# Attention and feed-forward block, eight more slots of lead for the row scores, six key tiles, untied weight loads, one staging tile

## The chip, the core and the metric

The kernel runs on one core of one Trainium2 chip. The core has a matrix engine (PE), a vector engine (DVE), a scalar engine (ACT), a general engine (POOL) and a sync engine (SP), which here issues every DMA. Each takes its instructions in order and waits on semaphores. Arithmetic is float32, and matrix products use the float32r form with operands split into a high and a low part. The metric is device time in microseconds (us) of one launch, lower is better.

## What is computed

A transformer block over 2048 rows of 576 features: a modulated layer norm, attention with 32 heads of 18 features, a residual, a second modulated layer norm, a feed-forward of 4608 features, a residual.

```python
mod = (silu(c) @ w_mod)            # sa, ca, ga, sb, cb, gb
h = layernorm(x) * (1 + ca) + sa
q, k, v = split_heads(h @ wqkv)    # 32 heads of 18
p = softmax(q @ k.T * 18 ** -0.5)
x = x + ga * (merge_heads(p @ v) @ wo)
h = layernorm(x) * (1 + cb) + sb
x = x + gb * (silu(h @ w1) @ w2)
```

## The kernel before

**Stages.** The 2048 query rows are cut into four blocks of 512. A block has eight quads, and a quad is four heads of one block. In the trace the stages are: the start (0 to about 152 us), the attention of block 0 (to about 618), the attention of blocks 1, 2 and 3 (to about 1197, 1715 and 2205), and a tail with the feed-forward of block 3. The output projection, second norm and feed-forward of a block (`post`, L888) are cut into filler pieces that run between the attention slots of the next block. In block 0 the filler is the remaining query and key projections (`qk_one`, L563, 24 of them, 14 matmuls each).

**Slots.** A quad has 32 slots. Each slot is done twice over, in two passes.

- Pass a, row scores (`slot_a`, L739, matmul at L735): two matmuls give the scores of 128 queries against 512 keys for two heads in banks `psa`, three of which exist, and DVE takes the row maximum of each (`mx`, L737). After the 32nd slot of a quad `max_a` (L749) joins the maxima and `max_rows` (L760) sends them by DRAM (`mscr`) into two spare rows of the quad's query tile `qt`. Eight slots share one chunk of 512 keys, held in two of four tiles `ka`.
- Pass b, exponentials (`slot_b`, L768, matmul at L785): two matmuls give the scores of 128 keys against 512 queries, less the row maximum through the two spare rows, in banks `psb`. ACT writes the exponentials to one of the tiles `pt`. The keys of a chunk of eight slots lie in two of four tiles `kb`.

Pass b of slot s runs beside pass a of slot s + `LEAD`, with `LEAD` 40, so the maxima of a quad are finished eight slots before its first exponential. The first 40 slots of pass a lie in the start. The last 40 slots of pass b have no pass a beside them.

**Values.** When both head pairs of a key tile (128 keys) have their exponentials, `pv` (L815) multiplies them with the values. Up to `PVMAX` = 5 key tiles go in one run. A key tile holds two `pt` tiles. There are seven `pt` tiles in block 0 and three more afterwards (`PB = 7, 10`, L60 and L865). `room` (L1508) keeps the planner from starting a slot when all are taken.

**Loads of keys.** `slot_load` (L717) loads `ka` and the query tiles, `slot_b` (L773) loads `kb`: in slot 8n + 2 and 8n + 4 the tiles of chunk n + 1. These take the place of chunk n - 1, which pass b left at slot 8n. A query tile (`load_quad`, L681, three buffers) asks first that the filler has projected its heads (`need`, L675): what is missing runs at once, without slots between.

**Weights.** `weights` (L643) prepares split weights on their first use. It loads half a tile to `raw` (three buffers), POOL writes high and low parts, and the result is stored in DRAM (`w1s`, `w2s`, `wos`) at the next call (`store_rest`, L638). For the first layer and the output projection this happens in block 0 through a staging tile `we` (`early`, L633, two buffers, 41 tiles). For the second layer it happens on first use by the feed-forward of block 0, which runs in the attention of block 1, straight into the tiles `w2t` (five buffers). POOL there does three passes for each half: times the gate (L654), cast (L655), difference (L656). Later blocks load the stored parts (L647). `after_pe` (L457) makes a DMA wait for the last exponentials' score matmul that stands before it in the program. It is on all first loads (L652) and their stores (L641), and not on the loads of stored parts.

**Order.** The order on PE is written by a planner with fixed costs (`Plan`, L99, and the loop from L1498): it chooses among a slot, a run of values and a piece of filler. Filler is paced evenly over the slots: in block 0 over 2 x 236 half slots from the loop's start (L1496). The other engines and SP get their order from the framework's scheduler: an instruction is placed when, by the scheduler's own clock, what it needs is ready, with program order as priority. The start has a list scheduler of its own (`Start`, L191) with priorities for all engines.

```python
        if j == 0:
            if s >= 8 and s % 8 in (2, 4):
                load_k("b", s // 8 + 1, s % 8 // 2 - 1)
...
            after_pe(nc.sync.dma_start(raw, src[:, cs]))
```

Of the kernel before, what the change touches and what calls it, by code (L numbers as in the profile page):

```python
# [18 lines left out]
P = 128  # L19
# [17 lines left out]
SCALE = DH ** -0.5  # L37
EPS = 1e-5
QM, KM, XM = 0, 1, 2
LEAD = 40  # L40
CH = 4


# [13 lines left out]
LP0 = 1000  # L57
REST = (16, 8, 0, 0)
LP = 2000
PB = 7, 10  # L60
PVMAX, PVMIN = 5, 3
QKB = 3
GS = 2
# [27 lines left out]
def f(ap):  # L91
    return ap.bitcast(F32)
# [98 lines left out]
class Start:  # L191
# [18 lines left out]
    def dma(self, size, fn, deps=(), prio=0, take=(), free=()):  # L210
        return self.add("D", size / self.RATE, fn, deps, prio, take, free)
# [128 lines left out]
def tile_adaln_block(ctx: ExitStack, tc: tile.TileContext, x, wqkv, wo, w1, w2, c, wfirst, wcol, out):  # L340
# [12 lines left out]

    at1 = ctx.enter_context(tc.tile_pool(name="at1", bufs=1))
    kas = [at1.tile([P, 512], F32R, name=f"ka{i}") for i in range(4)]
    kbs = [at1.tile([P, 512], F32R, name=f"kb{i}") for i in range(4)]

    ident = const.tile([P, P], F32, name="ident")
    make_identity(nc, ident)
# [97 lines left out]
    def after_pe(ins):  # L457
        if state["pe"] is not None:
            tc.add_manual_dep(ins.ins, state["pe"].ins.name, SYNC, reason="its turn by the plan")
# [171 lines left out]
                        fill.add(200, lambda a=mt_: mod_piece(*a), mode="full")  # L631

    def early(src, scr, gate=None):  # L633
        weights(mp["e"].tile([P, 2, 640], F32R, tag="w", name="we", bufs=2)[:, :, :src.shape[1]], src, scr, True, gate)

    stores = []

    def store_rest():  # L638
        while stores:
            w, scr = stores.pop()  # L640
            after_pe(nc.sync.dma_start(f(scr), f(w)))  # L641

    def weights(w, src, scr, first, gate=None):  # L643

        store_rest()
        if not first:
            nc.sync.dma_start(f(w), f(scr))  # L647
            return
        n = w.shape[2] // 2
        for cs in (slice(0, n), slice(n, 2 * n)):  # L650
            raw = mp.get("p", mp.get("e")).tile([P, 320], F32, tag="raw", name="raw", bufs=3)[:, :n]
            after_pe(nc.sync.dma_start(raw, src[:, cs]))  # L652
            if gate is not None:
                nc.gpsimd.tensor_tensor(raw, raw, gate[:, cs], op=ALU.mult)  # L654
            nc.gpsimd.tensor_copy(w[:, 1, cs], raw)  # L655
            nc.gpsimd.tensor_tensor(w[:, 0, cs], raw, f(w[:, 1, cs]), op=ALU.subtract)  # L656
        stores.append((w, scr))
# [39 lines left out]
    def load_k(ring, n, hp):  # L697
        i, kc = divmod(n, NKEY)
        if i >= NQ:
            return  # L700
        kt_ = (kas if ring == "a" else kbs)[n % 2 * 2 + hp]
        h = 4 * (i % NQUAD) + 2 * hp
        for j in range(2):
            nc.sync.dma_start(f(kt_[64 * j:64 * j + 54, :]),
                              f(kscr[(h + j) * DH:(h + j + 1) * DH, :, kc * 512:(kc + 1) * 512].rearrange("d c s -> (d c) s")))
        quads.setdefault(i, {})[ring, kc, hp] = kt_
# [9 lines left out]

    def slot_load(s):  # L717
        i = s // 32
        if s % 32 == (22 if i == 0 else 14) and i + 1 < NQ:
            load_quad(i + 1)  # L720
        n, w = divmod(s, 8)
        if w == 1:
            if s == LEAD + 1:
                load_k("a", n + 1, 0)
            load_k("a", n + 1, 1)
        elif w == 5:
            load_k("a", n + 2, 0)
# [40 lines left out]
    def slot_b(s, j):  # L768
        i, w = divmod(s, 32)
        kt, hp = divmod(w, 2)  # L770
        t = quads[i]
        if j == 0:
            if s >= 8 and s % 8 in (2, 4):  # L773
                load_k("b", s // 8 + 1, s % 8 // 2 - 1)
            if w == 0:
                t["P"] = {}
            if w == 16 and i + 1 < NQ:
                load_v(i + 1)
            state["p"] += 1
            t["P"][kt, hp] = pts[0]  # L780
            pts.append(pts.pop(0))

        e = 1 - j
        ps = bank_b("psb")
        state["pe"] = mm(ps, lhsT=t["b", kt // 4, hp][64 * e:64 * e + 56, kt % 4 * P:(kt % 4 + 1) * P],  # L785
           rhs=t["q"][64 * e:64 * e + 56, hp, :], start=True, stop=True)
        nc.scalar.activation(t["P"][kt, hp][:, e, :], ps, AF.Exp, scale=SCALE)  # L787
        at = t.setdefault(("exp", kt), [])
        rel = plan.take("b")

        def done(at_):
            rel(at_)
            at.append(at_ + TR)
        plan.op("A", plan.t + TL - TS + 30, TEXP, done)
        if hp == 1 and j == 1:
            pend.append((i, t, kt, at))
# [324 lines left out]
    def start_tasks(st):  # L1121
# [282 lines left out]
        k_in = {}  # L1404
        ones_t = []
        t = dma(16e3, lambda: nc.sync.dma_start(f(oscr.rearrange("r (a s) -> r a s", a=NKT)), full[0:2, None, :].to_broadcast([2, NKT, P])), prio=4.2)
        for n in range(8):
            ones_t.append(dma(40e3, lambda n=n: nc.sync.dma_start(f(kbs[n // 2][64 * (n % 2) + 54:64 * (n % 2) + 56, :]), f(oscr[:, :512])), [t], 8.4))
        q_in = [dma(443e3, lambda: load_quad(0), stored[QM, 0, 0], 5.5)]
        for kc in range(4):  # L1410
# [3 lines left out]
        mm_t = None  # L1414
        for s in range(LEAD):
            i, w = divmod(s, 32)
            if s in (24, 32):
                kc = s // 8 - 3
                k_in[1, kc] = dma(443e3, lambda kc=kc: [load_k("a", 4 + kc, hp) for hp in range(2)], stored[KM, 0, kc] + stored[KM, 1, kc] + [mm_t, k_in[(0, 3) if kc == 0 else (1, 0)]], 10 if kc else 8.8)
            ka = tok("a", 2)  # L1420

            def both(s=s):
# [192 lines left out]
```

## Time and profile before

| what | value |
|---|---|
| runs | 2488.22, 2495.07, 2496.23 us, median 2495.07 |
| profiled execution | 2487.03 us, of which 2485.2 us is the span of its instructions |
| granted PE clock over the span | 0.977 |
| DMA | 459.56 MB, 185 GB/s on average |

The span is what the views of the profile cover. The remaining 1.8 us of the profiled execution lie around it. A row of a group gives its line in the kernel, engine, operation, result and operands, count, and after the bar the busy time in us, the mean duration in ns and the engine's idle time before it with what ended it. In the view of stretches each engine's busy time in us is followed by the count of instructions, and then the clock granted to PE (1.00 is full speed), the busy share of the 16 DMA engines and GB/s. In the timeline a row is start, duration, engine, line, operation, operands and the count of merged instructions, with the idle time before it in brackets.

### The profile page before, as it was taken

What the parts mean: (1) busy time and instruction counts of PE and PEld (TensorE: products, weight loads), DVE (VectorE), ACT (ScalarE), POOL (GpSimd) and SP (SyncE); (2) the same over time, 40 slices, a digit from 0 to 9 for tenths busy, and PEclk for the clock granted to TensorE, in tenths of its full rate; (3) what the DMA queues carried; (4) which work ended last, traced back from release to release, by engine and by line L of the source; (5) the groups of instructions that cost most, each with busy time, mean ns of one, the idle gap of its engine ahead of it and who ended that gap; (6) DMA issues with size and microseconds to landing.
All of it is one profiled execution on the core that took longest, in us unless ns stands there. A gap on an engine that the chain in (4) does not pass through costs nothing.

```text
span 2485.2 us, 52362 instructions
## 1 busy us (share of the span) xinstructions
PE 2369.4 (95%) x19952; PEld 1625.0 (65%) x19952; DVE 1785.8 (72%) x3110; ACT 1483.6 (60%) x2736; POOL 631.1 (25%) x763
## 2 busy tenths in 40 slices
PE   6999998998999999999999999999999999989999
PEld 5863343433666667666667767776676677678988
DVE  8887786887777778777788777887888778234333
ACT  5246675776566666666577677776677667732121
POOL 5213343421343444344221111112211111120000
PEclk9999998999999999998999999999999999999999
DMA  7767776755355565555455555444654454326563
GB/s 251 247 199 237 255 256 219 260 192 181 128 168 174 176 198 182 172 167 170 158 184 166 187 177 174 165 157 160 209 180 159 158 182 165 131 102 238 173 219 119
DMA packets 208003, 459.56 MB, mean 185 GB/s; under 512 B 32010, under 2 KB 68266, under 8 KB 207754
## 3 DMA queue, kind: packets, MB, share of 16 engines
q1 hardware_dynamic: 207754, 456.21, 55.2%
q8 instruction: 160, 2.62, 0.4%
q14 instruction: 89, 0.73, 0.1%
HBM read 365.07 MB, written 86.33 MB: 182 GB/s over the span
## 4 chain that ended last, share of the span: by engine, by line
PE 79%; DMA 7%; DVE 5%; POOL 3%; ACT 2%; issue 2%; SPq 1%; POOLq 0%; ACTq 0%; DVEq 0%
PE ps L483 24%; PE psv L822 16%; PE psa L735 12%; PE ps L477 10%; PE psb L785 8%; DMA raw<-in_w 4%; PE psqk L569 3%; DVE mx L737 2%; PE psv L483 2%; PE psp L483 1%; DMA kb<-kscr 1%; POOL raw L654 1%; PE psqk L483 1%; POOL w2t L655 1%; POOL w2t L656 1%
## 5 line engine op out<-in xcount | busy, mean ns | idle before, releaser
L737 DVE TENSOR_REDUCE mx<-psa 128x1 f32<-128x512 f32 x2048 | 1320.8, 684 | 364.6 <-PE psb L785 206.9
L787 ACT ACTIVATE pt<-psb 128x512 f32<-128x512 f32 x2048 | 1131.1, 598 | 554.6 <-PE psb L785 350.0
L785 PE MATMUL psb<-qt,kb 56*128 56x512 f32 x2048 | 760.6, 431 | 29.1 <-DMA kb<-kscr 9.9
L735 PE MATMUL psa<-ka,qt 54*128 54x512 f32 x2016 | 704.7, 422 | 9.8 <-DVE mx L737 8.1
L735 PEld LDWEIGHTS psa<-ka,qt 54*128 54x128 f32 x2016 | 339.3, 189 | 308.9 <-DVE mx L737 207.6
L822 PE MATMUL psv<-pt,vt 128*32 128x512 f32 x4096 | 518.8, 610 | 1.0 <-ACT ov L826 0.9
L483 PE MATMUL ps<-w2t,g 64*128 64x288 f32 x4992 | 428.6, 299 | 26.0 <-POOL w2t L655 15.2
L483 PEld LDWEIGHTS ps<-w2t,g 64*128 64x128 f32 x4992 | 395.2, 190 | 65.5 <-POOL w2t L655 18.6
L785 PEld LDWEIGHTS psb<-qt,kb 56*128 56x128 f32 x2048 | 357.4, 188 | 74.5 <-ACT pt L787 35.7
L483 PE MATMUL ps<-hh,w1t 64*128 64x512 f32 x2160 | 397.3, 393 | 1.8 <-DVE x L928 1.5
L483 PEld LDWEIGHTS ps<-hh,w1t 64*128 64x128 f32 x2160 | 246.5, 185 | 36.8 <-DVE mx L737 7.5
L1048 POOL TENSOR_TENSOR g<-etmp,g 128x512 fp32r<-128x512 f32 x108 | 138.0, 1300 | 425.7 <-ACT g L1047 337.3
L822 PEld LDWEIGHTS psv<-pt,vt 128*32 128x32 f32 x4096 | 99.6, 109 | 216.8 <-issue 211.5
L932 POOL TENSOR_TENSOR x<-x,gt 128x288 f32<-128x288 f32 x116 | 93.2, 804 | 527.1 <-ACT gt L931 527.1
L483 PE MATMUL ps<-hl,w1t 64*128 64x512 f32 x864 | 199.5, 391 | 0.0
L928 DVE TENSOR_TENSOR x<-ps,x 128x288 f32<-128x288 f32 x184 | 83.8, 456 | 122.3 <-PE ps L477 76.2
L477 PE MATMUL ps<-w2t,g 128*128 128x288 f32 x960 | 132.6, 298 | 7.4 <-ACT g L1047 5.9
L477 PEld LDWEIGHTS ps<-w2t,g 128*128 128x128 f32 x960 | 130.2, 190 | 9.9 <-ACT g L1047 6.3
L483 PEld LDWEIGHTS ps<-hl,w1t 64*128 64x128 f32 x864 | 107.1, 186 | 9.1
L1044 ACT ACTIVATE eq<-ps 128x512 f32<-128x512 f32 x36 | 21.6, 600 | 146.3 <-PE ps L477 146.3
L477 PE MATMUL ps<-hh,w1t 128*128 128x512 f32 x360 | 106.9, 390 | 0.5 <-DVE hh L414 0.5
L654 POOL TENSOR_TENSOR raw<-raw,gb 128x288 f32<-128x288 f32 x72 | 61.5, 868 | 164.1 <-DMA raw<-in_w 164.1
(139 smaller groups left out, 2045.3 us busy)
## 6 DMA issues: line engine op xcount, KB each, us to landing
w1t<-w1s SPq DMA_DIRECT2D x144, 640.0 KB
w2t<-w2s SPq DMA_DIRECT2D x108, 576.0 KB
kb<-kscr SPq DMA_DIRECT2D x512, 108.0 KB
ka<-kscr SPq DMA_DIRECT2D x504, 108.0 KB
w1s<-we SPq DMA_DIRECT2D x36, 640.0 KB
w2s<-w2t SPq DMA_DIRECT2D x36, 576.0 KB
vt<-vscr SPq DMA_DIRECT2D x32, 608.0 KB
qt<-qscr SPq DMA_DIRECT2D x128, 108.0 KB
```

Of the source, the lines that this page charges most:

```text
L477: mm(self.ps[late], lhsT=lhsT, rhs=rhs, start=(i == 0), stop=(i == self.n - 1))
L483: done = mm(self.ps[g], lhsT=lhsT[rows], rhs=rhs[rows], start=(s == 0), stop=(s == 2 * self.n - 1))
L569: mm(qk_ps[0], lhsT=w[b][:, kt, :], rhs=(hTl if a else hTh)[:, kt, n * 512:(n + 1) * 512], start=(i == 0), stop=(i == 13))
L654: nc.gpsimd.tensor_tensor(raw, raw, gate[:, cs], op=ALU.mult)
L735: mm(ps, lhsT=t["q"][64 * j:64 * j + 54, hp, stt * P:(stt + 1) * P], rhs=t["a" if ("a", kc, hp) in t else "b", kc, hp][64 * j:64 * j + 54, ...
L737: return lambda: nc.vector.tensor_reduce(t["mx"][:, 2 * j + hp, stt, kc:kc + 1], ps, axis=AX.X, op=ALU.max)
L785: state["pe"] = mm(ps, lhsT=t["b", kt // 4, hp][64 * e:64 * e + 56, kt % 4 * P:(kt % 4 + 1) * P], rhs=t["q"][64 * e:64 * e + 56, hp, :], s ...
L787: nc.scalar.activation(t["P"][kt, hp][:, e, :], ps, AF.Exp, scale=SCALE)
L822: mm(t["ps"][32 * h:32 * h + 32, :], lhsT=t["v"][:, c0:c0 + 32], rhs=t["P"][kt, h // 2][:, h % 2, :], start=(kt == 0), stop=(kt == NKT - 1 ...
L928: nc.vector.tensor_add(c["x1"][j][:, hs], ps, c["x1"][j][:, hs])
L932: nc.gpsimd.tensor_add(c["x1"][j][:, hs], c["x1"][j][:, hs], t)
L1048: (nc.vector if last else nc.gpsimd).tensor_tensor(g[:, 1, :], t, f(g[:, 0, :]), op=ALU.subtract)
```

## The change

`LEAD` goes from 40 to 48: 48 slots of pass a are in the start, and the key chunk of slots 48 to 55 is loaded there too (`k_in[1, 2]`, with changed priorities). The query tile of quad 2 is asked for in slot 58 instead of 46.

There are six `kb` tiles, a ring of three chunks, and the loads in slots 8n + 2 and 8n + 4 are those of chunk n + 2. Four more small loads write the rows of ones.

First loads of second-layer weights and all stores of split weights lose `after_pe`. The first loads of the first layer and the output projection keep it (`tie`).

The staging tile `we` has one buffer instead of two, and there are nine `pt` tiles instead of ten after block 0.

```diff
--- before.py
+++ after.py
@@ -37,7 +37,7 @@
 SCALE = DH ** -0.5
 EPS = 1e-5
 QM, KM, XM = 0, 1, 2
-LEAD = 40
+LEAD = 48
 CH = 4
 
 
@@ -57,7 +57,7 @@
 LP0 = 1000
 REST = (16, 8, 0, 0)
 LP = 2000
-PB = 7, 10
+PB = 7, 9
 PVMAX, PVMIN = 5, 3
 QKB = 3
 GS = 2
@@ -353,7 +353,7 @@
 
     at1 = ctx.enter_context(tc.tile_pool(name="at1", bufs=1))
     kas = [at1.tile([P, 512], F32R, name=f"ka{i}") for i in range(4)]
-    kbs = [at1.tile([P, 512], F32R, name=f"kb{i}") for i in range(4)]
+    kbs = [at1.tile([P, 512], F32R, name=f"kb{i}") for i in range(6)]
 
     ident = const.tile([P, P], F32, name="ident")
     make_identity(nc, ident)
@@ -631,25 +631,24 @@
                         fill.add(200, lambda a=mt_: mod_piece(*a), mode="full")
 
     def early(src, scr, gate=None):
-        weights(mp["e"].tile([P, 2, 640], F32R, tag="w", name="we", bufs=2)[:, :, :src.shape[1]], src, scr, True, gate)
+        weights(mp["e"].tile([P, 2, 640], F32R, tag="w", name="we", bufs=1)[:, :, :src.shape[1]], src, scr, True, gate, True)
 
     stores = []
 
-    def store_rest():
+    def weights(w, src, scr, first, gate=None, tie=False):
+
         while stores:
-            w, scr = stores.pop()
-            after_pe(nc.sync.dma_start(f(scr), f(w)))
-
-    def weights(w, src, scr, first, gate=None):
-
-        store_rest()
+            w_, scr_ = stores.pop()
+            nc.sync.dma_start(f(scr_), f(w_))
         if not first:
             nc.sync.dma_start(f(w), f(scr))
             return
         n = w.shape[2] // 2
         for cs in (slice(0, n), slice(n, 2 * n)):
             raw = mp.get("p", mp.get("e")).tile([P, 320], F32, tag="raw", name="raw", bufs=3)[:, :n]
-            after_pe(nc.sync.dma_start(raw, src[:, cs]))
+            ld = nc.sync.dma_start(raw, src[:, cs])
+            if tie:
+                after_pe(ld)
             if gate is not None:
                 nc.gpsimd.tensor_tensor(raw, raw, gate[:, cs], op=ALU.mult)
             nc.gpsimd.tensor_copy(w[:, 1, cs], raw)
@@ -698,7 +697,7 @@
         i, kc = divmod(n, NKEY)
         if i >= NQ:
             return
-        kt_ = (kas if ring == "a" else kbs)[n % 2 * 2 + hp]
+        kt_ = kas[n % 2 * 2 + hp] if ring == "a" else kbs[n % 3 * 2 + hp]
         h = 4 * (i % NQUAD) + 2 * hp
         for j in range(2):
             nc.sync.dma_start(f(kt_[64 * j:64 * j + 54, :]),
@@ -716,7 +715,7 @@
 
     def slot_load(s):
         i = s // 32
-        if s % 32 == (22 if i == 0 else 14) and i + 1 < NQ:
+        if s % 32 == (26 if i == 1 else 14) and i + 1 < NQ:
             load_quad(i + 1)
         n, w = divmod(s, 8)
         if w == 1:
@@ -770,8 +769,8 @@
         kt, hp = divmod(w, 2)
         t = quads[i]
         if j == 0:
-            if s >= 8 and s % 8 in (2, 4):
-                load_k("b", s // 8 + 1, s % 8 // 2 - 1)
+            if s % 8 in (2, 4):
+                load_k("b", s // 8 + 2, s % 8 // 2 - 1)
             if w == 0:
                 t["P"] = {}
             if w == 16 and i + 1 < NQ:
@@ -1404,7 +1403,7 @@
         k_in = {}
         ones_t = []
         t = dma(16e3, lambda: nc.sync.dma_start(f(oscr.rearrange("r (a s) -> r a s", a=NKT)), full[0:2, None, :].to_broadcast([2, NKT, P])), prio=4.2)
-        for n in range(8):
+        for n in range(12):
             ones_t.append(dma(40e3, lambda n=n: nc.sync.dma_start(f(kbs[n // 2][64 * (n % 2) + 54:64 * (n % 2) + 56, :]), f(oscr[:, :512])), [t], 8.4))
         q_in = [dma(443e3, lambda: load_quad(0), stored[QM, 0, 0], 5.5)]
         for kc in range(4):
@@ -1414,9 +1413,9 @@
         mm_t = None
         for s in range(LEAD):
             i, w = divmod(s, 32)
-            if s in (24, 32):
+            if s in (24, 32, 40):
                 kc = s // 8 - 3
-                k_in[1, kc] = dma(443e3, lambda kc=kc: [load_k("a", 4 + kc, hp) for hp in range(2)], stored[KM, 0, kc] + stored[KM, 1, kc] + [mm_t, k_in[(0, 3) if kc == 0 else (1, 0)]], 10 if kc else 8.8)
+                k_in[1, kc] = dma(443e3, lambda kc=kc: [load_k("a", 4 + kc, hp) for hp in range(2)], stored[KM, 0, kc] + stored[KM, 1, kc] + [mm_t, k_in[(0, 3) if kc == 0 else (1, kc - 1)]], 10 if kc == 2 else 8.8)
             ka = tok("a", 2)
 
             def both(s=s):
```

## Prediction

> **What bounds the kernel now.** I read the whole span first, then the stages.
>
> ```profile
> span 2485.2 us, 52362 instructions
> PE 2369.4 (95%) x19952; PEld 1625.0 (65%) x19952; DVE 1785.8 (72%) x3110; ACT 1483.6 (60%) x2736; POOL 631.1 (25%) x763
> core 0: us, PE busy (x) PEld busy (x) DVE busy (x) ACT busy (x) POOL busy (x), PEclk, DMA share, GB/s
> 0.00:152.00 152.00, 127.07 (x1131) 110.31 (x1132) 122.53 (x264) 53.17 (x91) 45.69 (x53) 0.99 0.74 240
> 152.00:600.00 448.00, 417.25 (x2411) 174.46 (x2407) 351.59 (x588) 305.10 (x586) 153.23 (x207) 0.96 0.71 231
> 600.00:618.00 18.00, 15.59 (x75) 5.88 (x75) 13.94 (x22) 12.94 (x24) 5.25 (x4) 0.87 0.49 145
> 618.00:1197.00 579.00, 545.28 (x4972) 382.43 (x4968) 427.56 (x720) 361.94 (x669) 238.86 (x307) 0.94 0.52 170
> 1197.00:1715.00 518.00, 513.13 (x5046) 366.77 (x5046) 419.01 (x717) 361.99 (x665) 92.28 (x94) 1.00 0.51 172
> 1715.00:2205.00 490.00, 484.90 (x4718) 342.85 (x4712) 340.82 (x591) 334.95 (x617) 84.57 (x86) 1.00 0.49 162
> ```
>
> PE carries the time. Blocks 1 (618 to 1197) and 2 (1197 to 1715) do the same matrix work, yet block 1 takes 61 us more. PE idles 33.7 us there against 4.9, and its clock is 0.94 against 1.00, which over 579 us is 35 us. Together 64, so idle time and lost clock explain it, each at full price. The change moves no matrix work out; it can only gain idle time and clock. So I went to PE's waits, then to the stretches in which the clock is at half behind them.
>
> ```profile
> PE ps L483 <- POOL w2t L655: 15.2, 9, 2.3
> PE psb L785 <- DMA kb<-kscr: 9.9, 5, 4.1
> PE psb L785 <- DMA qt<-mscr: 9.8, 2, 4.9
> PE ps L483 <- POOL w2t L656: 7.4, 16, 0.7
> PE psqk L569 <- ACT qt L573: 1.6, 1, 1.6
> 765.20:775.40 10.20, 8.00 (x43) 4.92 (x45) 2.34 (x4) 2.02 (x4) 5.17 (x6) 0.50 0.87 260
> 1123.60:1130.40 6.80, 6.23 (x40) 5.85 (x41) 2.89 (x5) 2.40 (x5) 3.53 (x4) 0.50 0.83 284
> 239.50:242.90 3.40, 3.40 (x16) 0.99 (x15) 0.76 (x2) 1.27 (x3) 1.31 (x2) 0.50 1.04 370
> 522.80:526.20 3.40, 3.40 (x16) 0.71 (x13) 1.37 (x3) 1.62 (x4) 0.00 (x0) 0.50 0.75 279
> 270.20:277.00 6.80, 5.99 (x20) 2.43 (x22) 1.29 (x2) 3.23 (x6) 2.19 (x3) 0.50 0.69 223
> 597.90:604.70 6.80, 4.42 (x16) 1.60 (x16) 1.30 (x2) 2.25 (x5) 0.00 (x0) 0.50 0.48 131
> 376.95 1.01 PE L785 MATMUL psb<-qt,kb 56*128 56x512 f32 x2 [2.71 <-issue]
> ```
>
> The rows of waits read: who waits for whom, us in total, times, longest. The stretches are first and last of three families. Behind the w2t waits lie five, 37.4 us in all; behind the kb waits four, 17.0 us; behind the qt waits three, 20.4 us. PE is busy through most of each, so half speed costs half: 18.7, 8.5 and 10.2 us. The last row is the first exponential of quad 4. The view names no releaser, but it stands where those of quads 2 and 8 wait for their maxima, so I count its 2.7 us there.
>
> **Untied second-layer loads.**
>
> ```profile
> POOL raw L654 <- DMA raw<-in_w: 164.1, 40, 11.0
> 750.51 1.61 SPq L652 DMA_DIRECT2D raw<-in_w  x3
> 759.32 3.21 POOL L654 TENSOR_TENSOR raw<-raw,gb 128x288 f32<-128x288 f32 x3 [6.70 <-DMA raw<-in_w]
> 762.95 0.77 PE L483 MATMUL ps<-w2t,g 64*128 64x288 f32 x2 [1.35 <-POOL w2t L655]
> 1316.08 2.30 SPq L647 DMA_DIRECT2D w2t<-w2s  x4
> ```
>
> Three raw loads are issued at 750.5, POOL gets them at 759.3, and PE stands at 762.95 for what POOL makes of them. POOL itself waits 164 us for such loads and is busy only 239 of block 1's 579 us, so it is late, not full. The last row shows what an untied load does: in block 2 the four w2t loads of a group go out together at 1316, though the program asks for them spread over two pieces of first-layer work. The scheduler places an untied load when its buffer is free. The raw loads should then run ahead by their three buffers, and POOL by the five w2t tiles. Nothing is added in their place; the stores lose their wait on PE too. At stake are 15.2 + 7.4 idle and 18.7 of clock, 41.3 us. Bounds 0 and 41.3. I take 35, for something else can come right behind a wait this short.
>
> On the clock a rule can be held against the rows. The Trainium skill, "TensorE: Matmul & The Clock Gate", Part 1, lets the clock fall to half after at least one idle window of about 3.4 us. By it, waits of at most 2.3 us would cost no clock. The stretches at 765 and 1123 stand at 0.50 behind just such waits, so here the measurement speaks against it; I keep its sum as a rival.
>
> **Six kb tiles.**
>
> ```profile
> L735 PE MATMUL psa<-ka,qt 54*128 54x512 f32 x2016 | 704.7, 422 | 9.8 <-DVE mx L737 8.1
> 462.50 4.89 DMA kb<-kscr
> ```
>
> A kb tile is free at slot 8n, and its new chunk is needed at 8n + 8 now, at 8n + 16 then. A slot in block 0 is 448 us over 256, 1.75 us, so the margin grows by 14 us; the longest wait is 4.1. The ka loads, asked for 11 slots ahead on the same queue, leave no DMA among the releasers of psa. At stake are 9.9 and 8.5, 18.4 us. Bounds 0 and 18.4. I take 12, since SP must also send them in time.
>
> **Lead of 48.**
>
> ```profile
> 262.44 5.50 DMA mscr<-mt
> 268.72 2.15 DMA qt<-mscr
> 146.75 0.39 PE L735 MATMUL psa<-ka,qt 54*128 54x512 f32 x2
> 148.85 0.39 PE L735 MATMUL psa<-ka,qt 54*128 54x512 f32 x2
> 147.18 1.29 DVE L737 TENSOR_REDUCE mx<-psa 128x1 f32<-128x512 f32 x2 [0.81 <-PE psa L735]
> 152.69 5.47 DVE L737 TENSOR_REDUCE mx<-psa 128x1 f32<-128x512 f32 x9 [0.93 <-PE psa L735]
> ```
>
> The maxima's way through DRAM takes 7.7 us of DMA in the first two rows, plus queueing. It gets eight slots, 14 us, more; the longest wait is 4.9. At stake are 9.8, 2.7 and 10.2, 22.7 us. Bounds 0 and 22.7. I take 17.
>
> The price is paid in the start. A slot of pass a comes there every 2.10 us, between two value projections, which end at about 152. Eight more slots come after them, and only DVE sets their pace: nine maxima in 5.47 us, 0.61 each, 9.7 us for sixteen. PE's share of that, eight pairs at about 0.23 (1.9 us), is saved from the loop. That leaves 8, and I add 2 for one half-speed stretch of 3.4 us, as PE is mostly idle meanwhile. Bounds: 0, if the 0.81 us gaps of DVE take them all, and 8 x 2.10 = 16.8. I take 10.
>
> In block 0 quads ask for their heads eight slots sooner, while the filler keeps its pace of 24 projections in 236 slots. Quad 3 needs five at slot 30 of the loop, paced 3.1 (before: slot 38, 3.9); quad 5 needs eleven at slot 94, paced 9.6 (before 10.4). So about two more projections run without slots between, each for a wait like the 1.6 on ACT. I take 3; bounds 0 and 6. The query tile of quad q + 3 now comes free two slots after it is asked for, and 16 slots before pass a uses it: nothing. The SP queue behind it holds key loads, whose margin is the one just added.
>
> **One staging tile, nine pt tiles, small loads.**
>
> ```profile
> L655 POOL CAST we<-raw x82: 421/452/459, 162.6 to 519.4; 128x320 fp32r<-128x320 f32 x72, 128x288 fp32r<-128x288 f32 x10
> L656 POOL TENSOR_TENSOR we<-raw,we x82: 782/872/1079, 163.5 to 520.5; 128x320 fp32r<-128x320 f32 x72, 128x288 fp32r<-128x288 f32 x10
> L641 SPq DMA_DIRECT2D w1s<-we x36: 319/343/1097, 169.5 to 477.1; - x36
> 447.35 7.63 DMA w1s<-we
> 1536.09 3.64 PE L822 MATMUL psv<-pt,vt 128*32 128x512 f32 x32
> L1408 SPq DMA_DIRECT2D kb<-oscr x8: 236/252/436, 32.0 to 35.2; - x8
> ```
>
> POOL's cast of the next tile now waits for the store of the last one. Queued behind it on POOL are the low parts of projections and their weights, for which PE has a projection's time and more. A tile takes POOL 2 x (0.45 + 0.87) = 2.65 us, then the store. Tiles come every (477.1 - 169.5) / 35 = 8.79 us. So a store of up to 6.1 us costs nothing. One lasted 7.63. Its 640 KB at block 0's mean 231 GB/s are 2.8 us, an estimate from those two rows. Between these I take 2 us; bounds 0 and 41 x (2.65 + 7.63 - 8.79) = 61.
>
> The longest run of values is 32 matmuls, four key tiles, so eight pt tiles. Counted through PE's timeline after 618 (slots issued less values done), at most nine are ever held: the tenth is not used. Nothing, at worst the one reordering of a run. The four loads of ones are 0.25 us each on SP, with nothing waiting: 0 to 1, taken as 0.
>
> **Sum.** -35 - 12 - 17 + 10 + 3 + 2 = -49 us. On the profiled execution's 2487.0 that is 2438. The median of the runs shown is 8.0 us above that execution; I carry this over: 2446.
>
> **Rivals.** *The w2t waits stay*, because SP, which takes its queue in order, reaches the loads no sooner. For it: the three loads at 750.5 went out at once, one behind another, and then took until 759. Against it: the row at 1316. Then -49 + 35 = -14, 2481.
>
> *Block 0 keeps its waits*: SP and the DMA engines, 0.71 busy there against 0.51 later, stay behind, and of the last two gains only quad 8 remains, three quarters of 4.9 + 3.4, 6 us. Against it: no psa waits for a DMA. Then -35 - 6 + 15 = -26, 2469.
>
> *Slower: the staging tile becomes the bound of block 0.* If a store takes over 6.1 us from POOL's last pass, the 41 tiles run later and later. POOL, SP behind the raw buffers, and last the key loads and projections follow them. At 7.63 us it costs 61 and the gains in block 0: -35 - 6 + 10 + 3 + 61 = +33, 2528. For it: that one store and the high DMA share. Against it: the 2.8 us, and that stores no longer wait for PE. The Trainium skill, "Trainium Kernel Development and Optimization", Best Practices, speaks on this side: it asks for double buffers so that DMA and compute overlap.
>
> *Short waits cost no clock* (the rule above, as a mechanism): only the waits of 4.1 and 4.9 us would. Then 0.85 x 22.6 + 0.65 x (9.9 + 3.4) + 0.75 x (12.5 + 6.8) = 42 gained, 15 paid, 2468.
>
> **How the numbers follow.** Forecast 0.62, w2t waits stay 0.14, block 0 keeps its waits 0.13, staging bound 0.09, no clock price 0.02. The forecast's own range is 2423 (all of the 82.4 gained, 10 paid) to 2474 (half gained, 20 paid). To hold eight in ten I reach from 2418 to 2486, over both faster rivals. Left out are the slower one and the tails. A measurement here tells about 0.3%, 7.5 us, from no change. Of the two rivals in the middle 0.04 and 0.02 fall within that band. So faster 0.62 + 0.10 + 0.11 + 0.02 = 0.85, same 0.06, slower 0.09.
>
> **What would show it.** Right: PE's waits for POOL w2t nearly gone and block 1's stage near 540 us at clock 0.98 or more; no kb and no qt from mscr among PE's waits; the loop beginning about 10 us later than at 152; POOL waiting for w1s stores a few us. Wrong: the raw loads still issued just ahead of their use; the waits of block 0 back under other names (wql, ka, psqk); or a start longer by over 17 us.

## The result, and the profile after

| | before | after |
|---|---|---|
| median of the runs taken beside each other | 2491.64 us (2485.26 to 2496.23, four runs) | 2456.03 us (2451.93 to 2461.08, four runs) |
| ratio | 1 | 0.986, 95% interval 0.9825 to 0.9894 |
| profiled execution | 2487.03 us | 2461.08 us |

The change gains 35.6 us by the medians, and 25.9 us between the two profiled executions. The predicted time, 2446, is 10 us too low; the range holds the measured one.

First the span, from the changed kernel's page:

```profile
span 2459.3 us, 52303 instructions
```

Its view of stretches comes next. From here on a stage begins with the first exponential matmul (`psb`) of a block in the timeline, those of quads 0, 8, 16 and 24. So the rows are the start and blocks 0, 1 and 2.

```profile
0.00:166.00 166.00, 139.58 (x1156) 116.69 (x1156) 134.55 (x285) 53.90 (x93) 45.57 (x55) 0.95 0.74 235
166.00:614.20 448.20, 416.45 (x2399) 175.89 (x2398) 343.39 (x583) 304.20 (x584) 154.10 (x210) 0.95 0.70 227
614.20:1140.40 526.20, 508.00 (x4801) 358.05 (x4803) 415.19 (x706) 353.81 (x652) 225.84 (x295) 0.98 0.55 180
1140.40:1654.70 514.30, 508.21 (x4994) 362.92 (x4992) 415.40 (x711) 358.40 (x658) 95.07 (x98) 1.00 0.51 172
```

The same view of the kernel before, cut at the same places of its work (its first exponentials come at 155.2, 600.3, 1158.7 and 1680.8 us):

```profile
155.20:600.30 445.10, 414.89 (x2398) 173.51 (x2398) 349.09 (x584) 304.39 (x584) 153.23 (x207) 0.96 0.71 232
600.30:1158.70 558.40, 527.00 (x4799) 368.08 (x4801) 418.26 (x704) 353.38 (x651) 222.63 (x285) 0.95 0.51 166
1158.70:1680.80 522.10, 514.02 (x4996) 366.42 (x4992) 415.09 (x711) 359.13 (x658) 104.39 (x111) 0.98 0.52 174
```

The start is 10.8 us longer (155.2 to 166.0), block 0 is 3.1 longer, block 1 is 32.2 shorter, block 2 is 7.8 shorter, and the rest stays. The gain lies wholly in blocks 1 and 2. Block 0, where most of what the six tiles and the longer lead were to remove stood, gained nothing. In block 1 PE does the same 4800 matmuls in 19.0 us less of busy time at a clock of 0.98 for 0.95: that is regained clock, and the other 13.2 us are idle time.

The waits of the changed kernel, those of PE, then of POOL, then of SP's queue:

```profile
PE psa L734 <- DMA ka<-kscr: 18.8, 10, 5.1
PE psb L784 <- ACT pt L786: 15.5, 20, 8.2
PE psqk L569 <- ACT qt L573: 4.3, 3, 1.6
```

```profile
POOL we L654 <- DMA raw<-in_w: 109.0, 19, 16.4
POOL we L654 <- DMA w1s<-we: 84.1, 17, 7.6
```

```profile
SPq L642 <- POOL we L655: 55.2, 24, 6.4
```

PE's waits for `w2t`, for `kb` and for `qt` from `mscr` are gone by name, all three. In their place stands a wait that the kernel before did not have, 18.8 us for the key tiles `ka` of pass a, and one of 8.2 us for ACT.

Where the `ka` waits come from can be followed at the longest. First SP's queue in the timeline, then the chain of waits that ends at PE:

```profile
337.18 0.36 SPq L649 DMA_DIRECT2D raw<-in_w  x1
343.35 0.34 SPq L642 DMA_DIRECT2D w1s<-we  x1
347.94 1.80 SPq L703 DMA_DIRECT2D ka<-kscr  x1
353.55 0.46 SPq L703 DMA_DIRECT2D ka<-kscr  x1
```

```profile
347.53 5.97 DMA qscr<-qkhl
353.50 0.05 issue
353.55 6.28 DMA ka<-kscr
359.97 0.76 PE psa L734
```

SP issues nothing from 337.54 to 343.35, where it stands for POOL at a store of `we`, one of the 24 such waits. What is behind that store goes out after it: a store of projected queries at 347.53, which takes 5.97 us and from which the chain leads on to the `ka` load of 353.55, and that load needs 6.28 us to land, so PE stands until 359.97. Then the clock follows, as in the kernel before. Of three stretches at half speed the first begins behind a `ka` wait of 2.1 us just before and takes in this one of 5.1, the second begins within the 8.2 us for ACT, and the third lies about the loop's beginning, 9.2 us of it in the start and 7.9 in block 0:

```profile
354.80:365.00 10.20, 5.06 (x19) 2.00 (x19) 3.17 (x5) 2.77 (x5) 2.48 (x4) 0.50 0.86 284
631.30:641.50 10.20, 6.16 (x37) 4.06 (x39) 2.36 (x3) 3.31 (x6) 8.91 (x13) 0.50 0.60 193
156.80:173.90 17.10, 17.03 (x38) 8.51 (x37) 13.45 (x23) 2.83 (x5) 0.15 (x2) 0.50 0.45 143
```

The wait for ACT, seen in ACT's timeline:

```profile
623.55 2.27 ACT L786 ACTIVATE pt<-psb 128x512 f32<-128x512 f32 x4 [0.86 <-PE psb L784]
633.35 0.63 ACT L903 ACTIVATE th<-ou 128x512 fp32r<-128x512 f32 x1 [7.53 <-DMA ou<-ov]
634.72 1.05 ACT L786 ACTIVATE pt<-psb 128x512 f32<-128x512 f32 x2
```

ACT takes its instructions in order, and a rounding of the attention output (`th`, the first work of `post` for block 0) stood 7.53 us for its load with the exponentials queued behind it.

### The profile page after: what moved, and what is told of

Read it like the earlier page. It is cut to its first block, busy times and chain, and to the rows that moved or that the text cites. A ratio compares the mean times of both kernels' runs of the same rounds, so it can differ in the third digit from the quotient of the medians.

```text
span 2459.3 us, 52303 instructions
## 1 busy us (share of the span) xinstructions
PE 2356.5 (96%) x19952; PEld 1618.1 (66%) x19952; DVE 1776.1 (72%) x3110; ACT 1483.0 (60%) x2736; POOL 625.6 (25%) x763
## 4 chain that ended last, share of the span: by engine, by line
PE 75%; DMA 6%; DVE 5%; ACT 2%; POOL 1%; issue 1%; SPq 1%; ACTq 0%; POOLq 0%; DVEq 0%
PE ps L483 25%; PE psv L821 16%; PE psa L734 11%; PE ps L477 10%; PE psb L784 8%; PE psqk L569 3%; DVE mx L736 2%; DMA ka<-kscr 2%; DMA raw<-in_w 2%; PE psp L483 1%; ACT pt L786 1%; PE psp L477 1%; DVE hh L408 0%; DMA qt<-qscr 0%; DVE ov L844 0%
## 5 line engine op out<-in xcount | busy, mean ns | idle before, releaser
L734 PE MATMUL psa<-ka,qt 54*128 54x512 f32 x2016 | 706.8, 423 | 32.4 <-DMA ka<-kscr 18.8
L483 PE MATMUL ps<-w2t,g 64*128 64x288 f32 x4992 | 409.2, 293 | 0.2
L483 PEld LDWEIGHTS ps<-w2t,g 64*128 64x128 f32 x4992 | 382.6, 186 | 29.4 <-DVE mx L736 6.7
L927 DVE TENSOR_TENSOR x<-ps,x 128x288 f32<-128x288 f32 x184 | 83.9, 456 | 123.4 <-PE ps L477 76.9
L1044 DVE SCALAR_TENSOR_TENSOR etmp<-etmp 128x512 f32<-128x512 f32 x108 | 74.3, 722 | 28.6 <-ACT etmp L1043 28.2
```

The costliest lines, as they stand in the source:

```text
L483: done = mm(self.ps[g], lhsT=lhsT[rows], rhs=rhs[rows], start=(s == 0), stop=(s == 2 * self.n - 1))
L734: mm(ps, lhsT=t["q"][64 * j:64 * j + 54, hp, stt * P:(stt + 1) * P], rhs=t["a" if ("a", kc, hp) in t else "b", kc, hp][64 * j:64 * j + 54, ...
L927: nc.vector.tensor_add(c["x1"][j][:, hs], ps, c["x1"][j][:, hs])
L1044: nc.vector.scalar_tensor_tensor(t, t, 1.0, u, op0=ALU.add, op1=ALU.mult)
```

## The experiments

Of each kernel the median, its range and the ratio to the kernel before with the 95% interval are given. The table at the end of this section has the stages of the profiled executions, cut as above (from unrounded times, so that a tenth can differ from the rows); block 3 ends and the tail begins with the last exponential matmul. One execution of each kernel was profiled, and executions of one kernel lie up to 9 us (the changed kernel) or 18 us (POOL issuing stores and loads) apart, so a few us between two stages are not established by themselves. In kernels made from the kernel before by adding two lines, lines stand two higher than there, three higher than in the changed kernel (psa L737, psb L787).

**The untied second-layer loads alone**, on the kernel before; the stores keep their wait.

```diff
-            after_pe(nc.sync.dma_start(raw, src[:, cs]))
+            ld = nc.sync.dma_start(raw, src[:, cs])
+            if "p" not in mp:
+                after_pe(ld)
```

> The kernel before, with one line changed: the first loads of second-layer weights no longer wait for PE; lead, kb tiles, staging and stores as before. By term 1 of the prediction block 1 (first exponential of quad 8 to that of quad 16, 558.5 us) falls by about 35, PE's waits for POOL w2t from 22.6 to below 3, and the other stages stay within 4 us: total about 35 us less than before. If term 1 was only partly the cause, block 1 falls by less than 20 and the rest of the 32 us of the changed kernel came from its other parts. If the wait of 8 us for ou behind the untied loads (seen at 635 us in the changed kernel) is theirs, it is here too, at about 620 us.

Measured 2440.14 us (2436.72 to 2442.79), 0.9795 (0.978 to 0.981). PE's waits and blocks 1 and 2 in the view of stretches:

```profile
PE psb L787 <- DMA qt<-mscr: 11.1, 3, 6.7
PE psb L787 <- DMA kb<-kscr: 8.3, 5, 4.2
PE psb L787 <- ACT pt L789: 6.9, 19, 1.2
```

```profile
600.10:1118.70 518.60, 507.55 (x4801) 355.01 (x4803) 417.04 (x704) 353.52 (x651) 222.86 (x291) 0.98 0.56 180
1118.70:1632.60 513.90, 508.46 (x4996) 362.12 (x4992) 415.25 (x711) 358.46 (x658) 94.25 (x96) 1.00 0.52 174
```

No wait for `w2t` is left. Block 1 loses 39.8 us, of which 19.4 are PE's busy time (the clock) and 20.4 idle; block 2 loses 8.2. The interval puts the gain at 47 to 55 us of the 2490.7 of the kernel before that ran beside it, more than the whole change gives, and it does not touch the interval of the changed kernel. All the rest of the change together costs some 16 us (2456.03 - 2440.14). The 8.2 us stall for ACT is not there: the longest wait for ACT is 1.2, so these loads alone do not make it.

**The stores tied again**, on the changed kernel.

```diff
-            nc.sync.dma_start(f(scr_), f(w_))
+            after_pe(nc.sync.dma_start(f(scr_), f(w_)))
```

> The changed kernel with all stores of split weights waiting for PE again. Theory 1 (untied stores make SP stand for POOL, and the ka loads stand behind them): SP's wait of L642 for POOL we, 55 us, falls to about 15, PE's waits of psa for ka loads, 18.8 us, fall below 6, and block 0 (first exponential to that of quad 8, 448 us) shortens by 15 to 25. Theory 2 (the one staging tile is what holds block 0): a later store makes POOL wait longer for it, block 0 stays or gets longer, up to 460. Theory 3 (kb loads that run ahead take the place of ka loads on SP): block 0 stays within 5 us and the ka waits stay near 19.

Measured 2448.93 us (2447.8 to 2456.35), 0.9842 (0.9821 to 0.9864). PE's and SP's waits:

```profile
PE psa L734 <- DMA ka<-kscr: 11.7, 5, 4.8
```

```profile
SPq L642 <- POOL we L655: 12.8, 13, 2.6
```

Block 0 is 7.7 us shorter than in the changed kernel, block 1 is 5.7 shorter. A tied store stands later in SP's queue, when POOL has nearly finished, so SP's standing for it there falls from 55.2 to 12.8 us. Part of it comes back at the raw loads, where SP stands 36.0 us for POOL instead of 14.9. Over block 0 all rows of SP's waits for POOL add up to 59.1 us, for 84.2 in the changed kernel and 29.2 in the kernel before. The `ka` waits fall with it. That is theory 1 in its direction, at a third to a half of the size that it gave block 0. The medians differ by 7.1, but the two intervals overlap.

**Two staging tiles again**, on the changed kernel; the room is found in three small tiles of the maxima, whose second buffers go.

```diff
-... name="we", bufs=1)[:, :, :src.shape[1]], src, scr, True, gate, True)
+... name="we", bufs=2)[:, :, :src.shape[1]], src, scr, True, gate, True)
-        negm = at1.tile([P, 4, NST], F32, name="negm", bufs=2)
+        negm = at1.tile([P, 4, NST], F32, name="negm", bufs=1)
...
```

> The changed kernel with two staging tiles, and one buffer instead of two for three small tiles of the row maxima to make room. Theory 2 (one staging tile): POOL's 84 us of waits for stores of w1s go, the ka waits of 18.8 us fall below 6 and block 0 falls from 448 to 425 to 435 us. Theories 1 and 3: the POOL waits go, but ka waits stay over 12 us and block 0 over 440.

Measured 2456.49 us (2450.84 to 2463.66), 0.9876 (0.9852 to 0.99). Waits of PE, POOL and SP:

```profile
PE psa L734 <- DMA ka<-kscr: 15.1, 12, 5.6
```

```profile
POOL we L654 <- DMA raw<-in_w: 198.4, 43, 16.3
```

```profile
SPq L642 <- POOL we L655: 51.0, 24, 5.9
```

POOL no longer waits for stores; it waits 198.4 us for raw loads instead, for 109.0 with one tile. Block 0 and block 1 are 7.0 and 5.0 us shorter in the profile, but the medians are the same. SP still stands 51.0 us for POOL at the stores. Theory 2 falls: POOL's waits for the stores went, and 15.1 us of `ka` waits stayed.

**SP relieved of the weights' transfers in block 0**, three kernels on the changed one: POOL issues the staging stores; POOL issues the stores and their raw loads; ACT issues both.

```diff
-            nc.sync.dma_start(f(scr_), f(w_))
+            (nc.gpsimd if "p" not in mp else nc.sync).dma_start(f(scr_), f(w_))
...
-            ld = nc.sync.dma_start(raw, src[:, cs])
+            ld = (nc.gpsimd if tie else nc.sync).dma_start(raw, src[:, cs])
```

The first kernel has the first pair of lines alone; the third has `nc.scalar` for `nc.gpsimd`.

> The changed kernel with the stores of staging tiles in block 0 issued by POOL instead of SP: same bytes, but SP no longer stands for POOL before a store. Theory 1 (SP stands for POOL at these stores, 55 us, and ka loads wait behind it): ka waits fall from 18.8 below 8 us, block 0 from 448 to 425 to 438. Theory 4 (the DMA engines are the limit of block 0, whoever issues): ka waits stay above 12, block 0 above 440.

> As the run before, and the first loads to the staging tile are issued by POOL as well. SP then has only keys, queries, values, projections and maxima in block 0. Theory 5 (any in-order wait on SP for the staging work is the cause: stores, raw buffers and the waits for PE): ka waits below 4 us, block 0 at 415 to 430. Theory 4 (DMA engines): block 0 above 440. If POOL itself becomes late, PE waits for wql or the row of projections, or q and k are stored late, and block 0 is above 448.

> The same loads and stores of block 0 issued by ACT. SP is relieved as with POOL, but ACT, which takes its queue in order, now stands for POOL and for PE before each, with exponentials behind it. Theory 5: ka waits below 4 us, but waits of psb for ACT pt rise from 15.5 us, to 30 or more; block 0 between 430 and 470.

Measured 2458.34 us (2456.52 to 2462.39), 0.9871 (0.9855 to 0.9887); 2446.55 us (2440.26 to 2458.25), 0.9827 (0.9794 to 0.9859); 2487.69 us (2479.7 to 2489.83), 0.9984 (0.997 to 0.9998). One row of PE's waits of each, in this order:

```profile
PE psa L734 <- DMA ka<-kscr: 19.5, 12, 3.5
```

```profile
PE psa L734 <- DMA ka<-kscr: 12.5, 10, 4.2
```

```profile
PE psb L784 <- ACT pt L786: 44.2, 43, 7.4
```

The first two do not relieve SP as they were meant to. Two rows of SP's waits, one of each:

```profile
SPq L649 <- POOL we L655: 56.3, 30, 4.6
```

```profile
SPq L596 <- POOL qkhl L574: 63.2, 14, 11.3
```

With the stores on POOL, SP stands for the same work of POOL one place further on, at the raw loads: 56.3 us, for 14.9 in the changed kernel. With the raw loads on POOL too, POOL is late with the projections, and SP stands for it at the stores of queries and keys. Over block 0 SP stands 83.9 and 97.3 us for POOL in these two, for 84.2 in the changed kernel. So that the `ka` waits stay does not speak against SP's standing for POOL as their source. Theories 1 and 5 are not tested by these kernels, and the reading of the chain above holds for that one place and is not shown for all ten. Theory 4, that the DMA engines are the limit, has both its signs here; the last kernel below bears on it. In the second kernel a third of the `ka` waits goes and block 0 gains 4.8 by the profile, which is of its slowest execution; its median is 9.5 below that of the changed kernel, but the intervals overlap. On ACT the result is worse: the `ka` waits vanish, but the transfers, issued in order among the exponentials, make PE wait 44.2 us for ACT, and block 0 takes 481.0, longer than the 430 to 470 expected.

**One kind of room taken back**, two kernels on the changed one: four `kb` tiles with their old loads, and a lead of 40.

```diff
-    kbs = [at1.tile([P, 512], F32R, name=f"kb{i}") for i in range(6)]
+    kbs = [at1.tile([P, 512], F32R, name=f"kb{i}") for i in range(4)]
...
-            if s % 8 in (2, 4):
-                load_k("b", s // 8 + 2, s % 8 // 2 - 1)
+            if s >= 8 and s % 8 in (2, 4):
+                load_k("b", s // 8 + 1, s % 8 // 2 - 1)
```

```diff
-LEAD = 48
+LEAD = 40
...
-        if s % 32 == (26 if i == 1 else 14) and i + 1 < NQ:
+        if s % 32 == 14 and i + 1 < NQ:
```

> The changed kernel with four kb tiles and loads one chunk ahead, as before; lead, ties and staging as changed. Theory 3 (the extra kb loads ahead displace the ka loads): the ka waits fall below 8 us and kb waits come back, 10 us or less; block 0 within 5 us of 448. Theories 1 and 2: ka waits stay above 12 us and kb waits come on top, block 0 at 455 to 470.

> The changed kernel with a lead of 40. By the terms of the prediction the loop begins 10 us sooner (about 155 instead of 166), and PE's waits for the row maxima come back, 10 to 13 us with up to 10 us of clock: the total is within 8 us of the changed kernel, rather slower. If the ka waits of block 0 come from the lead, they fall below 8 us; if from stores or staging, they stay above 12.

Measured 2460.45 us (2460.21 to 2463.94), 0.9885 (0.9868 to 0.9903), and 2458.34 us (2454.03 to 2462.98), 0.9874 (0.9852 to 0.9896). PE's longest row of waits for a transfer in each, and block 0 with a lead of 40:

```profile
PE psb L784 <- DMA kb<-kscr: 22.1, 9, 6.3
```

```profile
PE psb L784 <- DMA qt<-mscr: 37.1, 7, 12.7
```

```profile
154.60:616.40 461.80, 417.25 (x2398) 175.51 (x2398) 346.94 (x584) 304.37 (x584) 157.55 (x216) 0.93 0.70 225
```

In both the `ka` waits are gone. The 18.8 us for `ka` are 22.1 for `kb` with four tiles and 37.1 for `qt` with the old lead: by these rows, the transfer whose room was taken back is the one that PE is seen waiting for. The 37.1 are three times the 10 to 13 expected. Neither kernel differs from the changed one by more than the intervals. The lead of 40 shortens the start to 154.6 and gives it all back in block 0. SP stands for POOL in block 0 as long as in the changed kernel, 82.7 and 84.3 us.

**One kind of room added**, three kernels on the untied loads alone: lead 48 with its start loads; six `kb` tiles (with nine `pt` tiles and two staging tiles, the room coming from the three small tiles as above); lead 44.

```diff
-LEAD = 40
+LEAD = 48
...
-        if s % 32 == (22 if i == 0 else 14) and i + 1 < NQ:
+        if s % 32 == (26 if i == 1 else 14) and i + 1 < NQ:
...
-            if s in (24, 32):
+            if s in (24, 32, 40):
```

With a lead of 44 the second pair reads `if s % 32 == 14`.

> The kernel before with untied first loads of the second layer, and a lead of 48 (with the loads and priorities of the start that go with it); kb tiles, staging and stores as before. By term 3 of the prediction PE's waits for qt from mscr (11.1 us and 2.8 under issue) and some 10 us of clock go, and the loop begins 10 to 11 us later: total within 8 us of 2440. Theory B (SP's stream of loads runs late in block 0, and more room for one kind of load only moves PE's wait to the next): the qt waits go, but kb waits rise from 8.3 to 15 us or more, block 0 stays at 440 to 450, and the total is 2446 to 2456.

> The kernel before with untied first loads of the second layer and six kb tiles loaded a chunk further ahead; lead 40, two staging tiles, stores as before; nine pt tiles and one buffer for three small tiles of the maxima to make room. By term 2 the kb waits (8.3 us, some 10 us of clock) go and nothing is paid: total 2424 to 2434. Theory B: kb waits go, the waits for qt from mscr rise from 11 to 20 us or more, block 0 and 1 together stay within 5 us of 964, total 2436 to 2448.

> As e9 with a lead of 44 slots: half the price in the start (about 5 us) for four more slots, 7 us, of room for the maxima. If the waits for qt (longest 6.7 us) simply need that room, they fall below 3 us and the total is 2428 to 2438. Theory B: kb waits rise and the total is 2440 to 2448.

Measured 2442.25 us (2440.1 to 2443.44), 0.9813 (0.9783 to 0.9843); 2435.29 us (2425.53 to 2438.29), 0.9779 (0.9743 to 0.9816); 2430.62 us (2429.49 to 2433.99), 0.9766 (0.9731 to 0.9801). PE's waits of each in this order:

```profile
PE psb L787 <- DMA kb<-kscr: 19.8, 8, 8.6
PE psb L787 <- ACT pt L789: 13.3, 20, 5.2
```

```profile
PE psb L787 <- DMA qt<-mscr: 28.0, 5, 11.9
```

```profile
PE psb L787 <- DMA kb<-kscr: 18.8, 11, 7.0
PE psb L787 <- ACT pt L789: 8.5, 17, 3.2
```

The same seesaw from the other side: a longer lead removes the `qt` waits (2.1 us are left at 44) and `kb` grows from 8.3 to 19 or 20, six tiles remove the `kb` waits and `qt` grows from 11.1 to 28.0. The lead of 48 is no better in block 0 than 44 (431.7 and 431.2), but its start is 5.9 us longer and its block 1 5.5 longer. The longest wait for ACT grows with the lead: 1.2, 3.2, 5.2 us at 40, 44, 48.

But the names of the waits do not tell the whole. Block 0 with the untied loads at a lead of 40, then at 44:

```profile
154.60:600.10 445.50, 416.42 (x2398) 174.98 (x2398) 348.39 (x584) 304.42 (x584) 158.33 (x216) 0.95 0.71 233
159.60:590.70 431.10, 406.79 (x2398) 171.53 (x2397) 345.82 (x584) 303.82 (x584) 157.81 (x214) 0.98 0.72 239
```

Of the 14.4 us, 9.6 are PE's busy time, that is clock. So the longer lead shortens block 0 although the waits only change their name, and pays 5.0 of it in the start. Theory B's waits came in all three kernels, but its times did not: with a lead of 48 the total and block 0 were shorter than it said, with 44 the total was, and six tiles alone lie between the two forecasts.

**Both kinds of room, without the untied stores and the single staging tile**: the kernel with six `kb` tiles and untied loads, at a lead of 44. It has two staging tiles, and its stores keep their wait. Its diff is that of the two kernels above together.

> The kernel before with untied first loads of the second layer, six kb tiles loaded a chunk further ahead and a lead of 44; two staging tiles and tied stores as before. Both margins at once, with the two parts left out that cost block 0 time in e1 and e2. If the margins add up, kb and qt waits both fall below 4 us, no ka wait takes their place, and the total is 2416 to 2426. Theory B: the wait moves to ka, 10 us or more as in the changed kernel, block 0 stays near the 431 us of e11, and the total is 2427 to 2436.

Measured 2411.94 us (2407.83 to 2420.37), 0.9675 (0.9651 to 0.97): the fastest, below both kernels of this study and below the 2416 to 2426 expected. Its waits and the start and blocks 0 and 1:

```profile
PE psb L787 <- ACT pt L789: 7.7, 16, 2.7
PE psb L787 <- issue: 4.3, 2, 2.1
...
PE psa L737 <- DMA ka<-kscr: 3.1, 2, 1.7
```

```profile
0.00:161.10 161.10, 135.50 (x1148) 114.71 (x1148) 129.63 (x277) 54.08 (x93) 45.50 (x55) 0.97 0.74 237
161.10:579.70 418.60, 402.77 (x2399) 170.64 (x2398) 347.29 (x584) 303.69 (x584) 157.59 (x214) 0.99 0.73 246
579.70:1091.50 511.80, 503.84 (x4801) 353.68 (x4803) 416.21 (x704) 352.72 (x651) 223.36 (x292) 0.99 0.56 183
```

Here nothing of these stops PE for more than 2.7 us (the two waits without a named releaser stand before the first exponentials of quads 5 and 8; the 3.1 us for `ka` are two waits). Block 0 gains 26.5 us on the kernel before and runs at 0.99, for 0.96. So the terms of the prediction for block 0 are to be had, and the kernel that gets them differs from the changed one in four things: the tied stores, the second staging tile, a lead of 44 for 48, and the single buffers of the small tiles. Which of them does it was not separated. Against the untied loads alone, six tiles give 4.9 us, the lead of 44 gives 9.5 and both give 28.2: alone, each leaves PE waiting for the other's transfer. Neither of the single gains is clear of the noise; that of both is.

Two rivals can be held against this kernel. The `ka` tiles have no more room in it than in the changed one, yet PE waits 3.1 us for them and not 18.8, while SP stands for POOL 21.1 us in block 0 and not 84.2. So the two kinds of room do not bring the `ka` waits by themselves, at a lead of 44 at least. They came where SP stood long for POOL, at least 59 us in block 0 in every kernel that has them at 11 us or more. And the DMA engines (theory 4) were not the limit of block 0 as a whole: here they are 0.73 busy at 246 GB/s, for 0.70 at 227 in the changed kernel, whose block 0 is 29.6 us longer.

| kernel | start | block 0 | block 1 | block 2 | block 3 | tail |
|---|---|---|---|---|---|---|
| before | 155.2 | 445.0 | 558.5 | 522.1 | 513.3 | 291.2 |
| after | 166.0 | 448.1 | 526.2 | 514.3 | 513.0 | 291.6 |
| after, stores tied | 164.3 | 440.4 | 520.5 | 515.7 | 512.8 | 291.2 |
| after, two staging tiles | 167.8 | 441.1 | 521.2 | 513.5 | 513.0 | 291.3 |
| after, stores by POOL | 164.3 | 449.8 | 520.5 | 515.1 | 512.9 | 291.8 |
| after, stores and raw loads by POOL | 164.7 | 443.3 | 528.5 | 515.1 | 512.7 | 292.0 |
| after, both by ACT | 164.7 | 481.0 | 522.7 | 514.3 | 513.0 | 291.7 |
| after, four kb tiles | 166.0 | 448.5 | 527.4 | 515.6 | 513.2 | 291.5 |
| after, lead 40 | 154.6 | 461.7 | 521.1 | 516.5 | 513.6 | 291.7 |
| before, loads untied | 154.6 | 445.5 | 518.6 | 513.9 | 513.4 | 291.8 |
| the same, lead 48 | 165.5 | 431.7 | 526.2 | 513.9 | 512.9 | 291.6 |
| the same, six kb tiles | 155.0 | 443.0 | 516.7 | 516.6 | 513.5 | 291.7 |
| the same, lead 44 | 159.6 | 431.2 | 520.7 | 514.6 | 513.6 | 292.5 |
| six kb tiles and lead 44 | 161.1 | 418.5 | 511.8 | 515.4 | 513.7 | 291.4 |

## Why the prediction was right, and where it was not

The forecast's sign and its size to 10 us held, but through one term of gain only. By profiles the sum of -49 came out at -25.9.

**Untied second-layer loads: right, and too small.** Predicted 35 of 41.3 at stake. Alone they gave 47.4 between profiles (2485.2 to 2437.8), and PE's waits for `w2t` went to nothing. The 39.8 us of block 1 split into idle time and clock nearly as the prediction reckoned (22.6 and 18.7). The gain went past the bound by some 6 us, in block 2, which lost 8.2. The kernel before has two more stretches at half speed there, 1171.4 to 1181.6 and 1185.0 to 1191.8 us, around the last second-layer matmuls. They stand at waits that bear ACT's name (1.3 and 3.1 us), and the prediction's five do not have them. With the loads untied the clock in block 2 is 1.00 for 0.98. That those waits hung on the late loads too is likely by this, and not traced. In the changed kernel it was 32.2 in block 1 and 7.8 in block 2, where the wait of 8.2 us for ACT and its 10.2 us at half clock were new.

**Six kb tiles (-12) and the lead of 48 (-17): adding them to the staging edits is the step that failed.** The prediction read each wait's margin by itself, and took the `ka` loads for safe because no psa waited for a DMA in the kernel before. The `kb` and `qt` waits did go, as forecast, but block 0 did not get shorter. The transfers stand in one queue: with room for `kb` and `qt`, PE stood 18.8 us for the `ka` tiles in place of 9.9 + 9.8; with the room of either taken back, the `ka` waits went and that one's came. The two terms were not wrong as such: in the fastest kernel block 0 is 26.5 us shorter, near the 29 forecast, with the same `ka` tiles. What the prediction had wrong is that it added them to the staging edits of the same change, which it priced at 2 us and which made SP, the queue of all these loads, stand for POOL 84.2 us in block 0 instead of 29.2. How much of the loss is theirs, and how much that of 48 slots for 44, is open. Among its signs of being wrong was "the waits of block 0 back under other names (wql, ka, psqk)", and it is what came, as `ka`. The rival "block 0 keeps its waits" has the sum that was measured: it gave -26 on the profiled execution.

**One staging tile: its direction right, its size wrong; the untied stores: not costed.** The prediction gave 2 us for the tile, with a store of up to 6.1 us free, and said that POOL would wait a few us for the stores. POOL waited 84.1. In the profiles a second tile gave block 0 7.0 us back, but the medians did not move. Nor did the tile become the bound of block 0. Of the stores the prediction only said that they lose their wait. That wait had kept them behind the moment at which POOL is done: without it SP stood 55.2 us at them, for 12.8 tied, and tying them gave block 0 7.7 back by the profile, which the medians do not part from noise. What the two cost together stays partly open: both were never taken back at a lead of 48, and moving the stores to another queue did not take SP's standing for POOL away.

**The start: right.** Predicted +10, measured +10.8. The half-speed stretch there is 17.1 us long and not 3.4. In its 9.2 us before the loop DVE sets the pace, so it added little. In the 7.9 us behind, PE is busy throughout, so half speed costs up to half of them there, an estimate of 4 us that the prediction did not have. The bursts of projections came as three waits of 4.3 us for 1.6 in one, near the 3 forecast.

**The median over the profile.** The prediction carried over that the runs before lay 8.0 us above their profiled execution. After, the median lies 5.1 below its profiled one. So of the 23 us by which the sum missed, 13 are hidden in the comparison of medians: that the forecast time came within 10 us is to that extent luck.

**Clock and short waits.** The rival that short waits cost no clock falls: with the `w2t` waits, none over 2.3 us, out of block 1, PE's busy time for the same matmuls fell by 19.4 us. The rule of the Trainium skill, "TensorE: Matmul & The Clock Gate", Part 1, that an idle window of about 3.4 us comes before half speed, does not hold for these waits. PE was not idle through any such window: in the 3.4 us before each of the five stretches it was busy for 0.77 to 1.76 us, between several short waits.

**What stays open.** Why ACT's wait for the attention output grows with the lead is only argued: a longer lead puts the query and key loads of a quad nearer to the end of block 0, where the outputs are reloaded by the same queue. Lead 48 with everything of the fastest kernel, and one staging tile without the other edits, were not tried, and no kernel takes SP's standing for POOL away by itself.

## What to carry to other kernels

A wait that is removed on a shared in-order queue may only uncover the next transfer on that queue that comes late: read the room of all of them, those that show no wait too, and what else makes the issuing engine stand. Here two kinds of room gave 28.2 us together and 14.4 as the sum of each alone. An explicit wait on a store can be a good place in the queue rather than a cost; before it is taken away, look at whether the issuing engine will then stand at the store, and before it is moved, at whether the engine will stand at the next transfer instead. And when a bundle of edits gives less than its parts promise, try the surest part alone first: here one line gave more than the whole.

## What the runs showed of the hardware

Transfers issued from ACT among its activations cost this kernel far more than they relieved: PE waited 44.2 us for exponentials, and block 0 took 481.0 us, for 443.3 with the same transfers on POOL and 448.1 on SP.

PE's clock stood at 0.50 for 17.1 us about the end of the start. In the first 9.2 us of them DVE paced PE: 16 matmuls came one every 0.6 us, and the records, whose ends are modelled, still show PE busy in nearly all of that time. So the granted clock also falls where PE has sparse work and no wait of its matmuls is named. With a lead of 44 the stretch there was 10.2 us in the fastest kernel and 6.8 with the untied loads alone, and 3.4 in the kernel before, with a lead of 40.
